# Fused attention and gated MLP on one Trainium2 core: batch 0's softmax and first layer split by tokens in place of heads, and a new order of all instructions

## The chip, the cores and the metric

The kernel runs on one core of a Trainium2 chip. The metric is the time of one execution on the device in microseconds (us), lower is better. The kernel before was run three times: 360.33, 360.48 and 363.59 us, a median of 360.48 us. The execution that was profiled took 361.51 us, and its first to last instruction span 359.7 us.

The engines are named as the profile does: PE is TensorE's matmul, PEld its weight load, DVE is VectorE, ACT is ScalarE, POOL is GpSimd, and SP issues the DMAs.

## The reference

B = 8 batches, H = 8 heads of D = 64, S = 512 tokens, Ns = 32 state rows, d_model = H·D = 512, d_ff = 1024.

```python
scores = x @ state.T / sqrt(D);  a = softmax(scores)      # over the 32 state rows, per token and head
xread  = a @ state                                        # (B, H, 512, 64)
scores2 = state @ x.T / sqrt(D); a2 = softmax(scores2)    # over the 512 tokens
sread  = a2 @ x                                           # (B, H, 32, 64)
X = concat([xread, sread], axis=2)                        # 544 rows per head, then heads side by side
h = relu(X @ w_in)                                        # (B, 544, 1024)
conv = conv_w[0]*h[t-1] + conv_w[1]*h[t] + conv_w[2]*h[t+1]
out = (h * sigmoid(conv)) @ w_out                         # (B, 544, 512)
```

## The kernel before

**How the work is cut.** `xread @ w_in` is not made in two steps: for each batch and each half of d_ff, u = state @ w_in is formed first (128 rows, 4 heads x 32 state rows, for each of two groups g of heads), and the hidden layer of 128 features f is then ps_h = u^T a (`hidden`, one step i = 8·b + f for each batch b and feature block f, 64 steps). A step goes on through ReLU, three taps of the convolution, tanh for the sigmoid, the gate, and four matmul groups, one for each chunk of 128 tokens, with w_out (`project`). Products at full accuracy are made of three passes in fp32r, a high part and a low part of each operand (`PASSES`); batch 0's first layer and its steps with i below `WHOLE` = 4 run instead as plain f32 matmuls, since their operands then need no split. The state rows (sread) are gathered for four batches at a time and go through the layers as "tails" (`state_hidden`, `tail`); the last token chunk of batch 0 goes through `last_product`.

**Weights.** w_in and w_out come in 16 pieces of 512 KB (`w_load`, tile raw) and each is converted by two ACT operations (L237, L240) and three DVE operations (L243, L246, L254) before PE may read it. w_in's columns are cut into four blocks of 1, 1, 2 and 4 feature blocks (`BLOCKS`), so that `block_state` can form batch 0's u for the first features before all of w_in is there.

**Batch 0's softmax.** The other batches take the softmax over state rows with DVE transposes (`softmax`). Batch 0 uses PE to be sooner (`first_softmax`): the scores (4 heads x 32 state rows on the partitions, 512 tokens along the free axis, one PSUM bank for each group g of four heads) are flipped (`first_flip`, L451), DVE takes the maximum for each token and head (`first_top`, L455), PE spreads it back into the bank of the scores (`spread`, L461, 16 matmuls), ACT takes the exponential (`first_exp`, L470), PE sums (`first_sum`, L474), DVE adds and inverts (`first_norm`, L478 and L479), PE spreads the inverses (L461 again, 16 matmuls), and DVE multiplies (`first_div`, L485). This chain is walked twice, once for each group g of heads. A step of the first layer (`hidden`, L588) adds both groups up, so that it needs both.

**What sets the order.** Each engine executes its instructions in the order of the program. The program's order is a table of numbers, `ORDER`: every operation is first listed with what it reads and writes (`add`), and the table then says in which order the operations are emitted; "-k" stands for k matmuls that fill PE's time (`fill`, L209) and a "v" after a number moves that operation from ACT to DVE. `Plan.order` refuses a table in which an operation stands ahead of one that it needs by that list. Buffers are few (`SBUF`): one buffer for a batch's x (xx), four for its transpose (xt), six for raw weights. All loads and stores are issued by SP, in order.

## Time and profile before

| | |
|---|---|
| median of three runs | 360.48 us |
| the profiled execution | 361.51 us |
| its span, first to last instruction | 359.7 us |
| granted TensorE clock, mean over the span | 0.995 |
| PE busy | 351.5 us (98%) |
| DVE busy | 319.6 us (89%) |
| ACT busy | 248.0 us (69%) |
| POOL busy | 67.6 us (19%) |
| DMA | 35.05 MB, mean 97 GB/s |

Of the chain of work that ended last, 92% of the span is PE and 6% DMA. The busiest group is the second layer (L651, 173.7 us on PE), then the first layer of batches 1 to 7 (L593, 83.9 us). In the first 50 us the 16 DMA engines are busy for 0.81 to 1.03 of the time. A busy PE is not a PE at its peak: its records overlap, and the start-to-start distance of a group's matmuls tells more than their durations. ACT and DVE instructions of a row that are merged (x2) show two starts and one end, so that half of such a row is what one of them adds to the queue.

### The profile page before, as it was taken

To read this page: it belongs to the slowest core of one execution; us is meant where nothing else is said; L and a number is where in the kernel's file an instruction comes from. 1 tells how busy PE (TensorE), PEld (TensorE's weight loads), DVE (VectorE), ACT (ScalarE), POOL (GpSimd) and SP (SyncE) were. 2 spreads that over 40 slices of the span, in tenths; PEclk is the share of its full clock that TensorE was granted. 3 is DMA by queue.
4 is the path that set the end of the run, shared out by engine and by line. 5 is a ranking of instruction groups with operands and counts; after the bars stand their busy time and mean duration, and the time that the engine had idled before them with its cause. 6 is when DMAs were issued, how large, how long until landed. Compare 5 with 4: busy or idle time off the path is not lost.

```text
span 359.7 us, 6635 instructions
## 1 busy us (share of the span) xinstructions
PE 351.5 (98%) x2488; PEld 266.0 (74%) x2488; DVE 319.6 (89%) x568; ACT 248.0 (69%) x506; POOL 67.6 (19%) x159
## 2 busy tenths in 40 slices
PE   7899999999999999999999999999999999999996
PEld 6644545878687877878878887887878777888884
DVE  1979999989999999999999999999799979998941
ACT  2789998998776889675784757656665555566541
POOL 1003100291301222111021402402202320410000
PEclk9989999999999999999999999999999999999999
DMA  7999886200443032300100002010030010100014
GB/s 260 389 356 379 282 342 236 104 2 1 148 148 118 0 126 79 133 17 2 68 21 29 2 6 81 2 59 3 0 117 2 0 58 2 59 1 31 30 58 146
DMA packets 12817, 35.05 MB, mean 97 GB/s; under 512 B 1521, under 2 KB 3697, under 8 KB 11761
## 3 DMA queue, kind: packets, MB, share of 16 engines
q1 hardware_dynamic: 12784, 34.63, 26.9%
q8 instruction: 19, 0.31, 0.4%
q14 instruction: 14, 0.11, 0.1%
HBM read 25.71 MB, written 8.91 MB: 96 GB/s over the span
## 4 chain that ended last, share of the span: by engine, by line
PE 92%; DMA 6%; SPq 0%; ACT 0%; issue 0%; DVE 0%; ACTq 0%; DVEq 0%
PE acc L651 45%; PE ps_h L593 21%; PE ps_hs L574 4%; PE ps_h L588 4%; PE ps_u L508 4%; PE acc_t L651 3%; DMA raw<-w_in 3%; PE ps_r L341 2%; DMA xx<-xn 2%; PE ps_s L300 2%; PE acc_c L651 2%; PE ps_t L328 1%; PE acc L659 1%; DMA raw<-conv_w 1%; PE ps_s L461 1%; PE ps_u L527 0%
## 5 line engine op out<-in xcount | busy, mean ns | idle before, releaser
L651 PE MATMUL acc<-wo,g 128*128 128x512 f32 x708 | 173.7, 393 | 0.0
L651 PEld LDWEIGHTS acc<-wo,g 128*128 128x128 f32 x708 | 130.9, 188 | 34.0 <-issue 4.2
L593 PE MATMUL ps_h<-a,u 128*128 128x512 f32 x336 | 83.9, 391 | 0.0
L593 PEld LDWEIGHTS ps_h<-a,u 128*128 128x128 f32 x336 | 62.6, 188 | 13.7 <-DVE u L202 0.8
L603 POOL COPY h<-hs 128x1 f32<-128x1 f32 x56 | 32.4, 588 | 166.4 <-DVE t L633 138.2
L628 ACT ACTIVATE t<-t 128x512 f32<-128x512 f32 x64 | 40.2, 632 | 19.9 <-DVE t L624 19.6
L624 DVE SCALAR_TENSOR_TENSOR t<-h,cw,t 128x512 f32<-128x512 f32 (+1 forms) x64 | 47.3, 745 | 1.1 <-DVE t L619 0.5
L633 DVE SCALAR_TENSOR_TENSOR t<-t,h 128x512 f32<-128x512 f32 (+1 forms) x64 | 42.4, 668 | 6.6 <-ACT t L628 6.4
L619 DVE SCALAR_TENSOR_TENSOR t<-h,cw,t 128x511 f32<-128x511 f32 x64 | 46.8, 743 | 1.0 <-ACT t L188 0.8
L608 POOL COPY hs<-h 128x1 f32<-128x1 f32 x64 | 29.2, 475 | 95.6 <-ACT h L194 87.2
L194 ACT ACTIVATE h<-ps_h 128x512 f32<-128x512 f32 x54 | 32.4, 599 | 19.4 <-PE ps_h L593 12.7
L199 ACT ACTIVATE g<-t 128x512 fp32r<-128x512 f32 (+1 forms) x60 | 37.0, 620 | 9.2 <-DVE t L633 7.7
L202 DVE TENSOR_TENSOR g<-t,g 128x512 fp32r<-128x512 f32 (+1 forms) x60 | 40.0, 675 | 1.1 <-ACT g L199 1.1
L188 ACT ACTIVATE t<-h,cw 128x512 f32<-128x512 f32 x49 | 34.8, 724 | 4.2 <-DVE g L202 2.3
L665 ACT ACTIVATE o<-acc 128x512 f32<-128x512 f32 (+1 forms) x29 | 15.8, 554 | 6.8 <-PE acc L651 4.9
L202 DVE TENSOR_TENSOR u<-ps_u,u 128x512 fp32r<-128x512 f32 x28 | 18.8, 682 | 0.6 <-ACT u L199 0.5
L574 PEld LDWEIGHTS ps_hs<-sr,wi 128*128 128x128 f32 x128 | 16.6, 191 | 3.2 <-ACT t L188 0.8
L199 ACT ACTIVATE u<-ps_u 128x512 fp32r<-128x512 f32 x28 | 16.0, 598 | 2.5 <-PE ps_u L508 2.4
L574 PE MATMUL ps_hs<-sr,wi 128*128 128x128 f32 x128 | 17.0, 276 | 0.0
L237 ACT ACTIVATE hc<-raw 128x512 f32<-128x512 f32 (+1 forms) x17 | 11.3, 666 | 7.6 <-DMA raw<-conv_w 4.4
L588 PE MATMUL ps_h<-p,u 128*128 128x512 f32 x32 | 14.8, 599 | 0.0
L508 PE MATMUL ps_u<-wi,st 64*32 64x512 f32 x224 | 14.8, 598 | 0.0
(95 smaller groups left out, 404.5 us busy)
## 6 DMA issues: line engine op xcount, KB each, us to landing
xt<-xT SPq DMA_DIRECT2D x16, 512.0 KB, 6.9
xx<-xn SPq DMA_DIRECT2D x8, 1024.0 KB, 4.9
out<-o SPq DMA_DIRECT2D x27, 256.0 KB, 2.1
raw<-w_in SPq DMA_DIRECT2D x8, 512.0 KB, 7.9
raw<-w_out SPq DMA_DIRECT2D x8, 512.0 KB, 7.9
out<-o SPq DMA_DIRECT2D x8, 128.0 KB, 1.8
out<-o_t SPq DMA_DIRECT2D x8, 64.0 KB, 1.7
st<-stT SPq DMA_DIRECT2D x1, 448.0 KB, 9.3
```

The lines of the kernel that those rows point to most:

```text
L188: A.activation(dst, src, AF.Copy, scale=scale)
L194: A.activation(dst, src, AF.Relu, scale=0.5)
L199: A.activation(hi, src, AF.Copy)
L202: engine.tensor_tensor(lo, src, hi.bitcast(F32), op=ALU.subtract)
L574: PE.matmul(ps_hs[m, f][:, :NT], wi[:, k, f * P:(f + 1) * P], sr[m][:, k, :], start=(k == 0), stop=(k == NK - 1))
L593: PE.matmul(ps_h[i], u[j][:, g, fs], a[k][:, g, :], start=(n == 0), stop=(n == 3 * NG - 1))
L603: G.tensor_copy(hd[i][:, S:], hs[m, f][:, j, 1:2])
L619: V.scalar_tensor_tensor(t[:, 1:], h[:, :S - 1], cw[:, f, 0:1], t[:, 1:], op0=ALU.mult, op1=ALU.add)
L624: V.scalar_tensor_tensor(t[:, :n], h[:, 1:n + 1], cw[:, f, 2:3], t[:, :n], op0=ALU.mult, op1=ALU.add)
L628: A.activation(tt[i], tt[i], AF.Tanh, scale=0.25)
L633: V.scalar_tensor_tensor(tt[i][:, :n], tt[i][:, :n], 1.0, hd[i][:, :n], op0=ALU.add, op1=ALU.mult)
L651: PE.matmul(acc, g[j][:, cs], wo[:, k, f, :], start=(f == 0 and n == 0), stop=(f == NF - 1 and n == 2))
```

## The change

The change has three parts.

1. Batch 0's two walks through `first_softmax` are no longer the two groups of heads; they are the two halves q of the tokens (`HS` = 256 tokens), each with all heads. The load of x transposed for batch 0 is cut in the same way (`xt_load`), the scores of a half go into two banks of 256 columns (`first_scores`), scaling, exponential and maximum work on 256 columns of each group, the inverses are spread into the bank of the flips, and the division is one DVE operation on 2 x 256 columns for each half. The first layer of batch 0 is cut in two as well (`first_hidden`): the matmuls of a token half need the division of that half alone. Each matmul there has 256 columns, and there are twice as many.
2. `WHOLE` goes from 4 to 2: steps 2 and 3 of batch 0 now split gate and w_out and run their second layer in three fp32r passes.
3. The list of needs is made exact (`join` writes one column and no longer the whole tile h; `flip` no longer claims e2t; `block_state` and the softmax of batch 0 name what they share), and the table `ORDER` is another one throughout: 36 operations carry a "v" where 33 did, and 13 fill matmuls stand in it where 18 did.

The core of the diff:

```diff
+HS = S // 2
+HC = NCH // 2
-WHOLE = 4
+WHOLE = 2
 ORDER = """
-120 121 0 98 -10 123 99 100 101 102 8 103 9 124v -6 141 2 11 10 125 3 149 126 142 12 -1 143 150 151 13 127 14 4 15 131
+120 0 -7 123 125v 121 98 99 100 101 -2 124 102 103 14 142 126 143 16 132 -2 150 2 20 15 144 3 4 8 151 145 127 152 17 5
...
     def xt_load(i):
         b, g = divmod(i, NG)
+        if b == 0:
+            xts[i] = buf([P, NP, HS], F32, "xt", f"xt_{i}")
+            nc.sync.dma_start(xts[i], xT[b, :, :, g * HS:(g + 1) * HS])
+            return
...
+    def first_scores(q):
+        if q == 0:
+            at[0] = buf([P, NG, S], F32, "at", "at_0")
+        ps_s[q] = [bank(f"ps_s_0_{q}_{g}") for g in range(NG)]
+        for j in range(NP):
+            for g in range(NG):
+                half = slice(g * D, (g + 1) * D)
+                PE.matmul(ps_s[q][g][j * NS:(j + 1) * NS, :HS], st[half, j, :], xts[q][half, j, :],
+                          start=True, stop=True)
+
+    def half_of(t, q):
+        return t[:, :, q * HS:(q + 1) * HS]
...
-    def first_exp(g):
+    def first_exp(q):
         if not pa:
             pa.append(buf([P, NG, S], F32, "at", "p_0"))
-        A.activation(pa[0][:, g, :], ps_s[g], AF.Exp, scale=SCALE)
+        for g, t in enumerate(ps_s.pop(q)):
+            A.activation(half_of(pa[0], q)[:, g, :], t[:, :HS], AF.Exp, scale=SCALE)
...
-    def first_spread(g):
-        spread(g, ident, True)
-
-    def first_div(g):
-        V.tensor_tensor(pa[0][:, g, :], pa[0][:, g, :], ps_s.pop(g), op=ALU.mult)
+    def first_spread(q):
+        spread(lambda k: ps_x[q][:, k * P:(k + 1) * P], q, ident, True)
+
+    def first_div(q):
+        V.tensor_tensor(half_of(pa[0], q), half_of(pa[0], q),
+                        ps_x.pop(q).rearrange("p (g s) -> p g s", s=HS), op=ALU.mult)
...
-        if b == 0:
-            for g in range(NG):
-                PE.matmul(ps_h[i], u[0][:, g, fs], pa[0][:, g, :], start=(g == 0), stop=(g == NG - 1))
-            return
...
+    def first_hidden(f, q):
+        if q == 0:
+            ps_h[f] = bank(f"ps_h_{f}")
+        for g in range(NG):
+            PE.matmul(ps_h[f][:, q * HS:(q + 1) * HS], us[0, f // 4][0][:, g, f % 4 * P:(f % 4 + 1) * P],
+                      half_of(pa[0], q)[:, g, :], start=(g == 0), stop=(g == NG - 1))
...
-            r = [("at", "p"), ("pa", 0), ("pa", 1), ("u0", 0, f // 4), ("uk", f, 0), ("uk", f, 1)]
+            for q in range(2):
+                add("PE", "hidden0h", partial(first_hidden, f, q), w=[("ps", "h", i)],
+                    r=[("at", "p"), ("pa", q), ("u0", 0, f // 4), ("uk", f, 0), ("uk", f, 1)])
...
-            add("POOL", "pool", partial(join, i), r=[("hs", m, f)], w=[("h2", i), h])
+            add("POOL", "pool", partial(join, i), r=[("hs", m, f), h], w=[("h2", i)])
```

The table moves instructions on every engine. Three places matter below. The rows are the built program's own; in a name such as hc_2_191 the first number is the tile's own (the weight piece, batch or step) and the last one counts buffers.

ACT, in the softmax of batch 0. hc and raw are a weight piece (0 and 1 hold w_in's first two blocks, 2 and 3 the third, 4 to 7 the fourth), p is the softmax of batch 0, and e2 the exponential of the other softmax, that over tokens. Before:

```order
L237 ACTIVATE hc_3_251<-raw_3_241 128x512
L240 ACTIVATE raw_3_241<-raw_3_241 128x512
L319 ACTIVATE e2_1_254,s2_1_255<-at_0_158,nm2_1_232 128x512
L240 ACTIVATE raw_2_227<-raw_2_227 128x512
L240 ACTIVATE raw_7_303<-raw_7_303 128x512
L237 ACTIVATE hc_5_308<-raw_5_305 128x512
L470 ACTIVATE p_0_234<-ps_s_0_1_139 128x512
```

And now:

```order
L502 ACTIVATE p_0_216<-ps_s_0_0_0_132 128x256
L502 ACTIVATE p_0_216<-ps_s_0_0_1_133 128x256
L238 ACTIVATE hc_3_248<-raw_3_189 128x512
L502 ACTIVATE p_0_216<-ps_s_0_1_0_154 128x256
L502 ACTIVATE p_0_216<-ps_s_0_1_1_155 128x256
L241 ACTIVATE raw_3_189<-raw_3_189 128x512
L341 ACTIVATE e2_0_261,s2_0_262<-at_0_131,nm2_0_219 128x512
L238 ACTIVATE hc_1_271<-raw_1_212 128x512
L341 ACTIVATE e2_1_286,s2_1_287<-at_0_131,nm2_1_178 128x512
L241 ACTIVATE raw_1_212<-raw_1_212 128x512
```

The second exponential of p stood behind work on the fifth and sixth pieces that are loaded (7 and 5); now both halves' exponentials stand ahead of the fourth loaded piece (1).

PE, from the second spread of inverses to batch 0's first layer. ps_x and ps_s are what the inverses are spread into, ps_t the flip of e, ps_h the first layer of one feature block. Before:

```order
L527 MATMUL ps_u_2_1_341<-wi,st 32x256
L461 MATMUL ps_s_1_139<-ident,s_1_334 32x128 x16
L300 MATMUL ps_s_0_378<-xt_312,st 32x512
...
L588 MATMUL ps_h_411<-p_234,u_0_279 128x512 x2
L588 MATMUL ps_h_416<-p_234,u_0_279 128x512 x2
```

And now:

```order
L561 MATMUL ps_u_2_1_298<-wi,st 32x256
L492 MATMUL ps_x_168<-ident,s_0_294 32x128 x16
L492 MATMUL ps_x_182<-ident,s_1_324 32x128 x16
L561 MATMUL ps_u_1_0_353<-wi,st 32x128
...
L350 MATMUL ps_t_366<-ident,e_1_286 128x128 x4
L631 MATMUL ps_h_378<-p_216,u_0_275 128x256 x4
L631 MATMUL ps_h_397<-p_216,u_0_275 128x256 x4
```

Both spreads now stand next to each other, behind the products with the third block of w_in, and the scores of the next batch (8 matmuls, L300) have left the place ahead of the first layer.

DVE, near the 230th of its 570 rows, in the steps of batch 2 (t_16 to t_23). u1_4 and u1_3 are low parts of u for batches 4 and 3, g1 the low part of a gate. Before:

```order
L202 TENSOR_TENSOR g1_16_1746<-t_16_1504,g0_16_1745 128x512
L202 TENSOR_TENSOR g1_17_1776<-t_17_1621,g0_17_1775 128x512
L322 TENSOR_SCALAR s2_12_1612<-s2_12_1612 128x1
L323 RECIPROCAL s2_12_1612<-s2_12_1612 128x1
L202 TENSOR_TENSOR u1_4_0_1715<-ps_u_4_0_1_1717,u0_4_0_1714 128x512
L633 SCALAR_TENSOR_TENSOR t_19_1654<-t_19_1654,h_19_1627 128x512
```

And now:

```order
L203 TENSOR_TENSOR g1_16_1739<-t_16_1637,g0_16_1738 128x512
L732 SCALAR_TENSOR_TENSOR ss_0_0_1355<-hs_0_0_82,cw_76,ss_0_0_1355 128x128
L444 TENSOR_SCALAR s1_3_1741<-s1_3_1741 128x32
L445 RECIPROCAL s1_3_1741<-s1_3_1741 128x32
L203 TENSOR_TENSOR g1_18_1754<-t_18_1614,g0_18_1753 128x512
L448 TENSOR_TENSOR af_3_1516<-af_3_1516,s1_3_1741 128x1024
L203 TENSOR_TENSOR u1_3_0_1762<-ps_u_3_0_1_1764,u0_3_0_1761 128x512
```

Batch 3's softmax (af_3) and u now come here, ahead of the rest of batch 2; the last row frees the PSUM bank into which PE's second chunk of batch 2's step 16 goes.

More of the change, by code (lines that the diff above doesn't have):

```diff
@@ L456, in first_top, with first_flip, spread @@
+    def first_flip(q):
+        ps_x[q] = bank(f"ps_x_{q}")
+        for k, g, cs in lumps(q):
+            PE.transpose(ps_x[q][:, k * P:(k + 1) * P], at[0][:, g, cs], ident)
+    def first_top(q):
+        sm[q] = buf([P, NCH, 4], F32, "s1", f"m0_{q}")
+        V.tensor_reduce(sm[q].rearrange("p c h -> p (c h)"), ps_x[q].rearrange("p (k n) -> p k n", n=NS), axis=AX.X,
                         op=ALU.max, negate=True)
-    def spread(g, by, start):
-        for c in range(NCH):
+    def spread(dst, q, by, start):
+        for k in range(NCH):
@@ L460, in spread @@
             for h in range(4):
-                PE.matmul(ps_s[g][h * NS:(h + 1) * NS, c * P:(c + 1) * P], sm[g][:, c, h:h + 1].broadcast_to([P, NS]), by,
-                          start=start and c == 0, stop=c == NCH - 1, skip_group_check=not start)
-    def first_shift(g):
-        spread(g, eight, False)
-    def first_exp(g):
+                PE.matmul(dst(k)[h * NS:(h + 1) * NS, :], sm[q][:, k, h:h + 1].broadcast_to([P, NS]), by,
+                          start=start and k == 0, stop=k == NCH - 1, skip_group_check=not start)
@@ L468, in first_exp, with first_shift @@
+    def first_shift(q):
+        spread(lambda k: ps_s[q][k // HC][:, k % HC * P:(k % HC + 1) * P], q, eight, False)
+    def first_exp(q):
         if not pa:
             pa.append(buf([P, NG, S], F32, "at", "p_0"))
[L470 to L479 removed]
@@ new lines, in first_softmax @@
+    def first_softmax(q):
+        x, m, n, p, e = ("ps", "x", q), ("s1", "m0", q), ("s1", "s0", q), ("pa", q), ("at", "p")
+        s = [("ps", "s", 0, q, g) for g in range(NG)]
+        add("PE", "flip", partial(first_flip, q), r=[("scores", 0, q), ("at", 0)], w=[x])
+        add("DVE", "red", partial(first_top, q), r=[x], w=[m])
+        add("PE", "spread", partial(first_shift, q), r=[m, ("scores", 0, q)], w=s)
+        add("ACT", "exph", partial(first_exp, q), r=s + [e] * q, w=[p] + [e] * (not q))
+        add("PE", "sum4", partial(first_sum, q), r=[p, e], w=[x])
+        add("DVE", "norm0", partial(first_norm, q), r=[x], w=[n])
+        add("PE", "spread", partial(first_spread, q), r=[n], w=[x])
+        add("DVE", "tt", partial(first_div, q), r=[x, e], w=[p])
@@ L847, in fused_kernel @@
         else:
-            for g in range(NG):
-                first_softmax(g)
+            for q in range(2):
+                first_softmax(q)
     for q in range(len(BLOCKS)):
```

137 lines of the change are left out of this document (64 added, 73 removed), and 57 rows, old and new, of the table ORDER.

## The prediction

> **What bounds the kernel now.** I read the page's first part, then the chain that ended last, then the engines' busy time by stretch, and last the timeline of the first 24 us.
>
> ```profile
> PE 351.5 (98%) x2488; PEld 266.0 (74%) x2488; DVE 319.6 (89%) x568; ACT 248.0 (69%) x506; POOL 67.6 (19%) x159
> ```
>
> The chain, in order of time (start, length, what):
>
> ```profile
> 7.86 9.78 DMA raw<-w_in
> 17.71 0.67 ACT hc L237
> 18.39 0.49 ACT p L470
> 18.92 1.05 PE ps_x L474 x8
> 19.98 0.93 PE ps_u L527 x16
> 20.91 1.86 PE ps_s L461 x32
> 22.77 1.38 PE ps_s L300 x16
> 24.15 5.35 PE ps_h L588 x12
> ...
> 29.50 1.02 PE ps_s L300 x16
> ...
> 41.52 0.86 PE acc L659 x2
> ...
> 63.54 0.70 PE acc L651 x3
> ...
> 350.08 6.13 PE acc L651 x27
> ```
>
> From 24.1 us, where batch 0's first layer starts, to 356.2 us the chain is PE at the pace of its matmuls, but for one load of x during which PE is busy as well. So the time is a start of 24.1 us, 332.1 us of PE, and a tail of 3.5 us. The start is set by the second walk of batch 0's softmax: its exponential (L470) stands on ACT behind a weight piece that lands at 17.7 us.
>
> PE is not alone. By stretches (length, then busy time and instructions of PE, PEld, DVE, ACT, POOL; clock; DMA share; GB/s):
>
> ```profile
> 23.44:137.60 114.16, 113.85 (x1013) 77.40 (x998) 111.28 (x203) 98.81 (x204) 27.27 (x52) 1.00 0.45 161
> 137.60:356.20 218.60, 218.59 (x1217) 174.04 (x1215) 194.71 (x336) 133.89 (x271) 38.58 (x84) 1.00 0.11 38
> 20.10:23.50 3.40, 3.40 (x56) 1.61 (x48) 2.51 (x8) 2.88 (x8) 0.00 (x0) 0.50 1.02 340
> 16.70:20.10 3.40, 1.81 (x20) 1.57 (x28) 2.52 (x6) 2.38 (x5) 0.00 (x0) 1.00 1.03 413
> 13.30:16.70 3.40, 2.85 (x75) 2.15 (x74) 2.68 (x8) 3.09 (x6) 0.00 (x0) 1.00 1.02 397
> ```
>
> For the 114 us behind the softmax DVE is idle for 2.9 us only: it is as full as PE. Later it has 24 us to spare. And just before the first layer PE ran at half clock for 3.4 us, after a stretch in which it was busy for 1.81 of 3.40 us.
>
> **The change part by part.** *PE's work* is nearly the same. Steps 2 and 3 have 6 matmul groups in the second layer (3 chunks each); each goes from 0.86 us (L659 above) to 0.70 (L651), so 6 x 0.16 = 1.0 us less. The scores that stood ahead of the first layer (L300, 1.02 us at full clock) now stand behind its start: 1.0 us more. The split matmuls stream as many columns as before. So from the first layer's start on PE has the same 332 us, and **what counts is when the first layer starts, and whether DVE can follow.**
>
> *The start.* The rows for the walk:
>
> ```profile
> 8.11 0.68 ACT L237 ACTIVATE hc<-raw 128x512 f32<-128x512 f32 x1 [1.34 <-DMA raw<-w_in]
> 13.48 0.69 ACT L237 ACTIVATE hc<-raw 128x512 f32<-128x512 f32 x1 [0.71 <-DMA raw<-w_in]
> 14.63 0.71 ACT L319 ACTIVATE e<-at,nm 128x512 f32<-128x512 f32 x1
> 15.34 1.23 ACT L240 ACTIVATE raw<-raw 128x512 uint32<-128x512 uint32 x2
> 20.95 0.55 ACT L188 ACTIVATE u<-ps_u 128x256 f32<-128x256 f32 x2 [0.38 <-PE ps_u L527]
> ...
> 14.54 1.08 PE L461 MATMUL ps_s<-ident,s 128*32 128x128 f32 x32
> 17.48 0.63 PE L328 MATMUL ps_t<-ident,e 128*128 128x128 f32 x4 [1.27 <-DVE p L485]
> ...
> 17.85 1.29 DVE L254 SCALAR_TENSOR_TENSOR wi<-raw,hc 128x512 uint32<-128x512 uint32 x2
> 20.01 0.18 DVE L478 TENSOR_SCALAR s<-ps_x 128x16 f32<-128x16 f32 x1 [0.88 <-PE ps_x L474]
> 20.22 0.25 DVE L479 RECIPROCAL s<-s 128x16 f32<-128x16 f32 x1
> 20.39 0.69 DVE L243 TENSOR_SCALAR hc<-hc 128x512 uint32<-128x512 uint32 x2
> ```
>
> The first and the fourth weight piece landed at 8.1 and 13.5 us, the third therefore near 11.7. The queue of loads is as long as before, but batch 0's x comes in runs of a quarter of the length; I allow 0.5 us for that (bounds 0 and 1), so third at 12.2, fourth at 14.0. From the third landing ACT's rows are: one weight operation (0.57), two exponentials of 256 columns (0.55), a weight operation (0.56): 13.9. Then DVE: one 0.60 operation and two more for the third block (15.7), a 0.34 shift, two inversions of 0.4 each (20.01 to 20.39, L478 and L479; 16.8). ACT meanwhile takes an exponential of 0.7, a weight operation, another exponential and a weight operation: 16.45. DVE: two 0.60 operations for the fourth piece and a small pair of 0.3 (L322 and L323, 131.41 to 131.68 below): 18.3; the division of the first half 18.9, a shift, the division of the second 19.85. PE: the third block's products end at 16.2, spreads of 0.93 each (L461) from 16.5 to 18.4, the second block's products 18.7, a flip of 0.5: 19.2. ACT has seven more operations on u and weights behind 16.45 (2.55 us): 19.0. **So the first layer starts at 19.3 us if the clock is full**, its second half's division done at 19.85 in time for it. With the clock halved a spread takes 1.86, as in the chain above: the spreads end at 20.2, the products and the flip at twice their length at 21.2, and the division at 20.95. [...] I take the middle: first layer at **20.2**, division at **20.4** (19.3 and 19.85 to 21.2 and 20.95), against 24.1 and 23.4.
>
> [...]
>
> *DVE behind the start.* The new order asks DVE for rows 32 to 230, 199 instructions, before PE may go into the second chunk of batch 2 (the third place shown above). From starts of neighbours:
>
> ```profile
> 31.96 1.41 DVE L624 SCALAR_TENSOR_TENSOR t<-h,cw,t 128x511 f32<-128x511 f32 x2
> 129.03 1.22 DVE L406 TENSOR_TENSOR af<-af,m 128x1024 f32<-128x1024 f32 x1
> 130.16 0.68 DVE L313 TENSOR_REDUCE nm<-at 128x1 f32<-128x512 f32 x1
> 131.41 0.14 DVE L322 TENSOR_SCALAR s<-s 128x1 f32<-128x1 f32 x1
> 131.68 0.73 DVE L624 SCALAR_TENSOR_TENSOR t<-h,cw,t 128x512 f32<-128x512 f32 x1
> 134.19 1.29 DVE L202 TENSOR_TENSOR g<-t,g 128x512 fp32r<-128x512 f32 x2
> ```
>
> a 512-column operation with one tensor of work adds 0.60 (L202), a tap 0.66 (L624), one of 1024 columns 1.13 (129.03 to 130.16). The 199 are 63 x 0.60, 52 x 0.66, 20 x 1.14, 14 of 384 columns at 0.47 (three quarters and a little of 0.60), 11 shifts at 0.34, and 39 small ones of 6.6 us together: 112 us. PE at that place has 215 us of matmuls left. PE had the same left at 137.6 us before, and DVE had by then done 111.3 us of work since the division (first of the stretches above). So the new order wants about 0.7 us more of DVE by the same point of PE, the two splits of gates among it, and everything 3 us earlier. DVE gets there at 20.4 + 112 + its idle time: with the 2.9 us of before 135.3, with half of it 133.9. PE itself would be there at 20.2 + 113.5 = 133.7. I take 134.6, nearer to the idle time seen. **The gain is 137.6 - 134.6 = 3.0 us** (bounds: 4.8 with the early start and a DVE that keeps up; 0.6 with the late start and 4 us of idle time, 20.95 + 112 + 4 = 137.0).
>
> *The rest.* Behind 137.6 us DVE is free for 24 of 219 us, so PE's 218.6 us stand. At the end two of the four last copies now run on DVE beside ACT:
>
> ```profile
> 352.83 0.76 DVE L667 TENSOR_SCALAR o<-acc 128x256 f32<-128x256 f32 x2 [0.94 <-PE acc L651]
> 356.23 0.66 ACT L665 ACTIVATE o<-acc 128x256 f32<-128x256 f32 x2 [0.70 <-PE acc L651]
> ```
>
> one of 0.42 in place of two in 0.66: 0.2 us less. Waits of PE that an order never run has elsewhere, on ACT between 25 and 50 us above all, I put at 0.3 us (bounds 0 and 2; the order before had 0.3, below). The exact needs cost nothing: POOL is busy for 19%.
>
> **Sum:** -3.0 - 0.2 + 0.3 = -2.9 us. The span goes from 359.7 to 356.8, that execution from 361.5 to 358.6, and the median of 360.5, 1.0 below the execution profiled, to **357.6 us**.
>
> **Rivals.** *PE alone binds.* DVE's idle time before fell where it had nothing to do; if it shrinks as DVE gets behind and the clock stays full, the first layer starts at 19.3 and PE is at the place at 132.8: 4.8 + 0.2 less, 355.5 us. Against it: DVE was 97% busy in that stretch already.
>
> *The clock halves over the spreads.* Start 21.2, division 20.95; DVE 20.95 + 112 + 2.9 = 135.9, so 1.7 + 0.2 less and 0.3 more: 358.9 us. [...]
>
> *The single buffer of x.* PE's read of x (L341) stands in its queue, with all behind it; each load can be issued only when the read before it is through.
>
> ```profile
> 51.02 1.10 PE L341 MATMUL ps_r<-xx,e2t 128*32 128x64 f32 x64 [0.31 <-DMA xx<-xn]
> DMA to landing us min/median/max: 4.8/4.9/8.7
> ```
>
> By the matmuls between them, PE gives the loads about 9, 6.0 and 6.9 us in the new order (6 to 7 before). At the median nothing is late. At the worst time seen, 8.7 us, two are late by 2.7 and 1.8; with the first read, for which 8.7 MB must have landed some 8.8 us into the first layer, late by 2 as well, PE loses 6.5 us: 364 us, slower than before. It decides from a loss of 2.9. For it: DMA is full until 50 us and now wanted earlier. Against: in the trace of before the one that came late did so by 0.31 us, and the next two loads queue behind less than then.
>
> *The split doesn't bring the start forward*, because the first layer also needs u of its features, and these hang on weights, not on the softmax: no change, 360.4 us. Against: the four pieces have landed by 14.0.
>
> **How the numbers follow.** The forecast, DVE setting the pace behind an earlier start, gets 0.5, with its own range of 356.2 to 359; PE alone 0.2; the halved clock 0.16; x late 0.1; no earlier start 0.04. A measurement of this kernel tells about 1% from no change, 3.6 us: faster means below 356.9, slower above 364.1. Faster takes all of the first rival and a third of the forecast, 0.37; slower half of the third rival's chance less a little, 0.04; the rest, 0.59, is within 1%. The range that leaves out no more than 2 in 10 reaches from the first rival's 355.4 to 361.0, short of the worst case of x.
>
> **What would show it.** Right: L631 starts between 19.3 and 21.2 us with the exponentials of both halves before 14 us; DVE is idle for less than 3 us between the division and 135 us; PE waits for DVE near 130 us, for one or two us in all; PE's work from the first layer on is 332 us. Wrong: first layer behind 22 us (the start's sum fails); PE at its pace throughout with DVE in hand (first rival); half clock over L492 (second); PE waiting at L363 for xx (third); PE waiting for ACT between 25 and 60 us by more than 2 us (the term for other waits fails).

## The result, and the profile after

The changed kernel takes 359.72 us (median of 20 runs, 358.7 to 363.0) against 362.3 us for the kernel before on the same chip (20 runs, 359.7 to 365.6). The ratio is 0.994, with a 95% interval of 0.9914 to 0.9966: 0.6% less, some 2.2 us, or between 1.2 and 3.1 (the two medians lie 2.6 apart). The forecast was 2.9 us less, from a median of 360.48 that three runs had given; from there to 362.3 are 1.8 of the 2.1 us by which the forecast time of 357.6 lies too low. The profiled executions differ by less: 361.51 to 360.01 us, span 359.7 to 358.2. **So in the profile 1.5 us are gained where 2.9 were forecast,** and the question is where the rest of a start that came 3.7 us earlier went.

A part of the timed gain is the clock's. Each run has its mean granted clock on record, and 0.995 is what one stretch of 3.4 us at half clock leaves, as in the profile of the kernel before (20.1 to 23.5 us). The changed kernel's profile has one as well (15.1 to 18.5 us), and a mean of 0.993, since its clock falls again behind PE's last matmul (0.80 in the mean from 353.75 us to the end). Over all comparisons below, on several chips, the kernel before took 360.8 us in the 28 runs with a mean clock of 0.998 or more and 362.5 us in the 54 with 0.994 or 0.995; the changed kernel took 359.4 us in 11 runs and 359.9 us in 20 (0.992 to 0.995). These are medians without an interval. At full clock the gain is about 1.4 us, with one halved stretch 2.6: a halved stretch cost the kernel before 1.7 us and the changed one 0.5.

The first part of the page of the changed kernel:

```profile
PE 350.4 (98%) x2532; PEld 272.4 (76%) x2532; DVE 323.0 (90%) x574; ACT 248.5 (69%) x508; POOL 46.6 (13%) x159
```

PE is at 98% as before; such a share doesn't tell of 1 or 2 us. I therefore cut PE's time at two marks that both programs have: the first layer's first matmul (L631, before L588), and the first matmul of the state tokens (L609, before L574). By stretches (length, then busy time of PE, PEld, DVE, ACT, POOL; clock; DMA share; GB/s), first the kernel before, then the changed one:

```profile
24.08:62.48 38.40, 38.09 (x444) 18.14 (x437) 37.63 (x80) 36.98 (x80) 4.73 (x14) 1.00 0.86 311
62.48:356.20 293.72, 293.71 (x1777) 233.29 (x1775) 267.72 (x459) 195.72 (x395) 61.12 (x122) 1.00 0.14 50
```

```profile
20.37:59.97 39.60, 39.45 (x492) 25.59 (x491) 37.53 (x79) 37.76 (x85) 5.24 (x14) 1.00 0.94 355
59.97:353.72 293.75, 293.65 (x1777) 233.26 (x1776) 272.43 (x465) 197.48 (x395) 39.69 (x122) 1.00 0.14 49
```

Behind the state tokens both take the same 293.7 us. The first layer comes 3.71 us earlier, the stretch up to the state tokens is 1.20 longer, and behind PE's last matmul 4.5 us follow where there were 3.5: -3.71 + 1.20 + 0.03 + 0.98 = -1.50. The stretch that got longer is the one in which the loads run at 355 GB/s and 94% of the DMA engines' time, against 311 and 86% before.

The chain of waits of the changed kernel, where it answers to the one shown of before:

```profile
17.60 0.60 DVE wi L255
18.62 8.19 DMA xt<-xT
26.85 1.06 PE ps_s L305 x8
27.92 2.79 PE ps_h L631 x12
30.70 1.03 PE ps_r L363 x64
...
60.14 7.14 PE ps_hs L609 x64
...
134.06 1.13 DVE af L448
...
135.84 6.44 PE acc L689 x27
...
344.20 9.53 PE acc L689 x42
353.76 0.39 ACT o L703
354.18 0.42 DVE o L705
```

The chain does not begin at the first layer any more. It runs through a load of x, issued at 18.62 us behind a weight load that had waited for DVE, and landed at 26.8. DVE's softmax of batch 3 stands in it at 134 us, as forecast. The timeline shows what waits for loads around 25 us:

```profile
24.25 0.68 ACT L241 ACTIVATE raw<-raw 128x512 uint32<-128x512 uint32 x1 [1.10 <-DMA raw<-w_out]
24.99 0.71 ACT L189 ACTIVATE t<-h,cw 128x512 f32<-128x512 f32 x1
25.67 2.25 PE L305 MATMUL ps_s<-xt,st 64*32 64x512 f32 x16
25.73 0.75 DVE L657 SCALAR_TENSOR_TENSOR t<-h,cw,t 128x511 f32<-128x511 f32 x1 [1.14 <-ACT t L189]
26.85 0.15 PEld L305 LDWEIGHTS ps_s<-xt,st 64*32 64x32 f32 x8 [1.05 <-DMA xt<-xT]
30.63 0.47 PEld L363 LDWEIGHTS ps_r<-xx,e2t 128*32 128x32 f32 x29 [0.33 <-DMA xx<-xn]
```

Three engines wait for the queue of loads: ACT 1.10 us for a piece of w_out, DVE behind ACT 1.14, PE 1.05 for x. The matmuls' own row hides PE's wait (its ends are modelled: 16 matmuls in 2.25 us that otherwise take 1.02), the row of the weight loads shows it.

### The profile page after: what moved, and what is told of

It is laid out like the page before. It is cut to its first block, busy times and chain, and to the rows that moved or that the text cites. A ratio compares the mean times of both kernels' runs of the same rounds, so it can differ in the third digit from the quotient of the medians.

```text
span 358.2 us, 6725 instructions
## 1 busy us (share of the span) xinstructions
PE 350.4 (98%) x2532; PEld 272.4 (76%) x2532; DVE 323.0 (90%) x574; ACT 248.5 (69%) x508; POOL 46.6 (13%) x159
## 4 chain that ended last, share of the span: by engine, by line
PE 90%; DMA 4%; DVE 4%; issue 0%; ACT 0%; SPq 0%; DVEq 0%
PE acc L689 46%; PE ps_h L624 21%; PE ps_hs L609 4%; DMA xt<-xT 4%; PE acc_t L689 3%; PE ps_u L542 3%; PE ps_h L631 3%; PE ps_r L363 2%; PE ps_s L305 2%; PE ps_t L350 2%; PE acc_c L689 2%; PE acc L697 1%; DVE hc L247 1%; DVE wi L255 1%; DVE hc L244 0%
## 5 line engine op out<-in xcount | busy, mean ns | idle before, releaser
L689 PE MATMUL acc<-wo,g 128*128 128x512 f32 x726 | 179.0, 394 | 0.1
L689 PEld LDWEIGHTS acc<-wo,g 128*128 128x128 f32 x726 | 134.5, 188 | 33.5 <-issue 3.0
L624 PE MATMUL ps_h<-a,u 128*128 128x512 f32 x336 | 82.9, 390 | 0.0
L646 POOL COPY hs<-h 128x1 f32<-128x1 f32 x64 | 24.1, 390 | 191.5 <-ACT h L195 172.8
L189 ACT ACTIVATE t<-h,cw 128x512 f32<-128x512 f32 x47 | 33.5, 722 | 1.0 <-DVE g L203 0.8
L641 POOL COPY h<-hs 128x1 f32<-128x1 f32 x56 | 16.6, 312 | 75.1 <-DVE t L671 55.8
L238 ACT ACTIVATE hc<-raw 128x512 f32<-128x512 f32 (+1 forms) x17 | 11.6, 681 | 5.8 <-DMA raw<-conv_w 5.5
L609 PEld LDWEIGHTS ps_hs<-sr,wi 128*128 128x128 f32 x128 | 14.7, 192 | 1.0 <-ACT h L195 0.8
L631 PE MATMUL ps_h<-p,u 128*128 128x256 f32 x64 | 15.1, 386 | 0.0
L609 PE MATMUL ps_hs<-sr,wi 128*128 128x128 f32 x128 | 14.9, 276 | 0.0
L631 PEld LDWEIGHTS ps_h<-p,u 128*128 128x128 f32 x64 | 11.8, 190 | 4.0 <-issue 0.8
```

Source lines behind the costliest of these rows:

```text
L189: A.activation(dst, src, AF.Copy, scale=scale)
L609: PE.matmul(ps_hs[m, f][:, :NT], wi[:, k, f * P:(f + 1) * P], sr[m][:, k, :], start=(k == 0), stop=(k == NK - 1))
L624: PE.matmul(ps_h[i], u[j][:, g, fs], a[k][:, g, :], start=(n == 0), stop=(n == 3 * NG - 1))
L631: PE.matmul(ps_h[f][:, q * HS:(q + 1) * HS], us[0, f // 4][0][:, g, f % 4 * P:(f % 4 + 1) * P], half_of(pa[0], q)[:, g, :], start=(g == 0) ...
L689: PE.matmul(acc, g[j][:, cs], wo[:, k, f, :], start=(f == 0 and n == 0), stop=(f == NF - 1 and n == 2))
```

## The experiments

Each kernel's time stands against the kernel before, run beside it on the same chip. Of the kernel before a fifth to a half of the runs beside it were at full clock, and these are 1.7 us faster than those with one halved stretch, so a difference of a few tenths of a per cent between rows is not clear. For every profile I give the first layer's start, the stretch up to the state tokens, the stretch from there to PE's last matmul, and the tail behind it, all read like the stretches above (us):

```
                 start   to L609   to last PE   tail   time / before (95%)
before           24.08   38.40     293.72       3.5    1
changed          20.37   39.60     293.75       4.5    0.9940 (0.9914 to 0.9966)
after_again      19.85   40.37     293.77       4.5    0.9944 (0.9921 to 0.9967)
whole            20.08   42.68     293.75       4.5    0.9990 (0.9962 to 1.0018)
scores_later     20.47   40.18     293.76       4.5    0.9977 (0.9952 to 1.0002)
act_later        22.29   38.73     293.78       4.5    0.9945 (0.9918 to 0.9972)
loads_order      19.66   40.21     293.76       4.5    0.9926 (0.9899 to 0.9954)
half_loads       20.50   38.41     293.77       4.5    0.9904 (0.9868 to 0.9939)
dve_more         20.40   38.72     294.69       4.5    0.9965 (0.9938 to 0.9991)
dve_less         20.57   39.29     293.77       4.5    0.9944 (0.9914 to 0.9975)
best1            19.51   40.01     293.73       4.5    0.9925 (0.9894 to 0.9956)
before_exp       22.26   41.82     293.74       3.5    1.0005 (0.9969 to 1.0041)
before_half      22.54   38.15     293.77       3.5    0.9955 (0.9918 to 0.9991)
best2            19.80   41.50     293.77       4.8    0.9976 (0.9945 to 1.0006)
```

My first theory was the prediction's, refined: PE and DVE come to the place at 135 us nearly together, and each loses about a microsecond on the way. The rivals were that PE alone binds and that DVE alone does. The first four kernels were made for these.

**The changed kernel again.** No edit.

> The changed kernel once more, as the measure for the three beside it. In its profile the first layer started at 20.4 us, PE was at the place (second chunk of batch 2, behind DVE's low part of u for batch 3) at 135.8, and its last matmul ended at 353.7, 333.4 us behind the first layer's start. What hangs on the order of the work must come again: a wait of about 1.1 us of PE for a load of x behind the first layer's first matmuls, one of 1.1 us of ACT for a piece of w_out, 115.5 us from the first layer to the place. What hangs on the phase of the clock (half clock from 15.1 to 18.5 us) and on the last stores (4.5 us from the last matmul to the end) may differ. Time against the kernel before: 0.991 to 0.997.

PE's wait for x came again (1.0 us) and a second one with it (0.9 us, for batch 0's x); ACT's wait for w_out did not (it waited 0.5 us for a piece of w_in), and from the first layer to the place it took 116.3 us. What I had not expected: the clock stayed full (0.999 in the mean), the first layer started 0.52 us earlier, and the state tokens still came 0.25 us later (19.85 + 40.37 = 60.22, against 59.97). An earlier start that is worth nothing can be a sign of something that doesn't depend on the start.

**The first layer's matmuls whole.**

```diff
-            PE.matmul(ps_h[f][:, q * HS:(q + 1) * HS], us[0, f // 4][0][:, g, f % 4 * P:(f % 4 + 1) * P],
-                      half_of(pa[0], q)[:, g, :], start=(g == 0), stop=(g == NG - 1))
+            PE.matmul(ps_h[f], us[0, f // 4][0][:, g, f % 4 * P:(f % 4 + 1) * P], pa[0][:, g, :],
+                      start=(g == 0), stop=(g == NG - 1))
```

(all of it at q = 0; at q = 1 the function returns)

> The first layer's matmuls of batch 0 at 512 columns, as before the change, in place of two of 256; everything else as changed. Theory of two limits: PE and DVE come to the place within 0.4 us of each other, DVE the later; the 256-column matmuls (0.2325 us, against 0.4296 for 512) cost PE 0.8 to 1.1 us, but taking this back alone leaves DVE as it is: first layer to the place 115.2 to 115.5, time 0 to 0.3 us less. Theory that PE alone binds: the full price, place 0.8 to 1.1 us earlier, time 0.8 to 1.1 us less. Theory that the halves cost nothing: no change in the busy time of those matmuls (14.5 us).

All of these are wrong about the time, which went up by about 0.5% against the changed kernel. From matmul to matmul the halves take 0.216 us each (median in the changed kernel), the whole ones 0.429: the halves cost next to nothing (0.432 against 0.429). The 0.2325 us of my expectation lies above that median. The chain of this kernel shows one wait:

```profile
19.32 0.43 SPq L234
19.80 12.05 DMA xx<-xn
31.89 1.10 PE ps_r L363 x64
```

The read of batch 0's x (L363) starts when x has landed, 12 us after it was asked for. Why the loads of this version came so late is not shown; only that PE had to wait for them.

**The scores later, and ACT's work on w_out later.** In the table of the order 202 to 204 are the scores of batch 2 and their copies, 52 is ACT's rounding of the first w_out piece.

```diff
scores_later:
-192 200 202 203 521 43 531 493 502 204 522 532 503 48
+192 200 521 43 531 493 502 522 532 503 202 203 204 48
act_later:
-490 517 52 450 519 530 44 45 129 520 47 491 51 46 189
+490 517 450 519 530 44 45 129 520 47 491 51 46 52 189
```

> The scores of batch 2, for which PE waited about 1.1 us for a load of x at 25.7 us, stand behind the first layer's matmuls of step 1 (2.8 us later in PE's queue), and their two copies on ACT with them. Theory of two limits: PE's wait goes, but DVE still comes to the place as late, so time 0 to 0.3 us less. Theory that PE alone binds: 1.1 us less. If the copies come later for DVE's reduction of the maxima, DVE gets a new wait near 29 us: time the same or up to 0.5 us more.

> ACT's rounding of the first w_out piece, for which ACT waited 1.1 us at 24.25 us and with it DVE 1.14 us at 25.7 for ACT's multiplication by the taps, stands three operations later in ACT's queue. Theory of two limits: DVE's idle time goes (1.1 us less of it up to 30 us), and then PE's own losses bind: first layer to the place 114.9 to 115.2, time 0.3 to 0.6 us less. Theory that DVE alone sets the place: place 1.1 us earlier, time 1.1 us less. Theory that PE alone binds: 0 to 0.35 us less.

Without its place in PE's queue the wait for x was gone at 25 us, but DVE had a new one of 1.85 us (for the copies of these scores) and the stretch was no shorter, 40.18 us. With ACT's rounding moved, the stretch was 38.73 us, but behind a start of 22.29: there the clock was halved for 6.8 us ahead of it. Start and stretch together, the state tokens come at 60.65 and 61.02 us. So far five profiles of the changed order had starts from 19.85 to 22.29 us, 2.4 us apart; but for `whole` (62.8) they reached the state tokens between 59.97 and 61.02, and in all five PE's read of batch 0's x started within 0.1 us of its landing. From there on all take 293.75 to 293.78 us, whatever happened ahead. That speaks against the theory of two limits at the place: DVE's and PE's losses on the way to 135 us would have to show behind the state tokens. The new theory: **the loads set the pace up to the state tokens.** Its rival was still DVE.

**Loads and DVE set against each other.** `half_loads` leaves out half of the bytes of x for batches 1 to 7 and of the other layout of x; `dve_less` leaves out a tap; `dve_more` does four operations twice.

```diff
half_loads:
-        nc.sync.dma_start(xts[i], xT[b, :, 2 * g:2 * g + 2, :])
+        nc.sync.dma_start(xts[i][:, :1], xT[b, :, 2 * g:2 * g + 1, :])
-        nc.sync.dma_start(xxs[b], xn[b])
+        nc.sync.dma_start(xxs[b][:, :2], xn[b, :, :2])
dve_less, in before(i):
+        if 8 <= i < 12:
+            return
dve_more, in w_low(f):
-        low(wo[:, 1, f, :], whole[f], wo[:, 0, f, :])
+        for _ in range(2 if 2 <= f < 6 else 1):
+            low(wo[:, 1, f, :], whole[f], wo[:, 0, f, :])
```

> The changed kernel with half of the x of batches 1 to 7 and half of the other layout of x left out (each load has half the bytes, and the matmuls read the half that is there twice), so that every instruction is as before but the loads are lighter. Theory of loads: x for the scores of batch 2 lands about 1.2 us earlier, batch 0's other layout 2 to 3 us earlier; PE waits for neither, L609 comes at 58.2 to 58.9 us, and the time falls by 1 to 1.8 us. Theory of DVE: 0 to 0.6 us less (only what ACT and DVE wait for w_out at 24 us). If the loads were no limit at all: no change.

> The first of the two convolution taps of steps 8 to 11 is left out (part of the computation: these four steps lack a tap), 4 x 0.66 = 2.6 us less of DVE's work between 65 and 110 us. Theory that DVE alone sets the place: PE there 2.0 to 2.6 us earlier, and the time as much less. Theory that PE and DVE are level there: PE's wait of 0.36 us goes and no more, 0.2 to 0.4 us less. Theory of loads: 0 to 0.4 us less, since PE's work between L609 and the place is what it is.

> Four of DVE's operations on w_out (the low parts of pieces 2 to 5, 0.6 us each, near 56 to 70 us) are done twice, with the same result: 2.4 us more of DVE's work before the place. Theory that DVE sets the place: 2.4 us less the 1.1 us that it idles behind them at 111 and 120 us, so PE at the place 1.3 to 2.4 us later and the time 1.3 to 2.4 us more. Theory of loads, with DVE in hand behind 60 us: less than 0.5 us more.

With the light loads the stretch fell to 38.41 us, within 0.01 of what it took in the kernel before, and the time to 0.9904 (four runs; the interval overlaps with that of the changed kernel):

```profile
20.50:58.91 38.41, 38.41 (x492) 25.52 (x491) 37.47 (x79) 37.70 (x85) 5.26 (x14) 1.00 0.70 232
58.91:352.68 293.77, 293.66 (x1777) 233.14 (x1776) 272.61 (x465) 197.43 (x395) 39.65 (x122) 1.00 0.12 39
```

That is what the theory of loads says, at the lower end of its numbers (1.1 us in the profile), and DVE's work is the same 37.5 us as in the changed kernel. But the loads of one profile differ from those of the next: `dve_more`, whose loads are whole and in the changed order, took 38.72. So the reading rests on more than one pair. Without a wait PE reads batch 0's x 9.07 us behind the first layer (`half_loads`, 20.50 to 29.57). These are the profiles with PE's order unchanged (us):

```
                 start   x landed   read of x   L609
half_loads       20.50   27.88      29.57       58.91
dve_more         20.40   29.73      29.77       59.12
dve_less         20.57   30.48      30.53       59.86
changed          20.37   30.57      30.63       59.97
after_again      19.85   30.63      30.67       60.22
act_later        22.29   31.60      31.64       61.02
```

With whole loads the read begins within 0.06 us of the landing in all five, and the state tokens follow the read by 29.3 to 29.6 us in all six. Whether the first layer starts at 19.85 or at 22.29, what arrives at L609 arrives when x does.

With a tap left out in four steps (DVE's work behind the state tokens falls from 272.43 to 270.16 us), PE reached the place in the same time behind the state tokens, 75.84 us against 135.84 - 59.97 = 75.87; in the stretch up to the place, and in DVE's timeline at 111 us, first of `dve_less`, then of the changed kernel:

```profile
59.86:135.70 75.84, 75.77 (x511) 58.94 (x510) 71.83 (x119) 61.90 (x121) 12.81 (x41) 1.00 0.23 77
```

```profile
108.75 0.71 DVE L664 SCALAR_TENSOR_TENSOR t<-h,cw,t 128x512 f32<-128x512 f32 x1
111.37 0.69 DVE L673 SCALAR_TENSOR_TENSOR t<-t,h 128x512 f32<-128x512 f32 x1 [1.91 <-ACT t L668]
```

```profile
111.49 0.69 DVE L671 SCALAR_TENSOR_TENSOR t<-t,h 128x512 f32<-128x512 f32 x1 [0.58 <-ACT t L666]
```

DVE waits 1.91 us there in place of 0.58: it has nothing to do until PE and ACT bring the next step. So DVE does not set the place. It is not far from it either: of 2.4 us more in `dve_more` (two of the four operations stand ahead of the state tokens), 0.94 came out behind them (293.75 to 294.69). That is between what the two theories expected, under 0.5 and 1.3 or more.

**Another order of loads.** Of the table's numbers 200 is a load of x for batch 2, 44 the last piece of w_in, 50 and 56 the first two of w_out, 122 the other layout of x for batch 0; ACT's 52 moves as above.

```diff
-199 13 50 448 27 34 ... 517 52 450 519 530 44 45 129 520 47 491 51 46 189 192 200 202 ... 56 122 137
+199 200 13 448 27 34 ... 517 450 519 530 44 50 122 45 129 520 47 491 51 46 52 189 192 202 ... 56 137
```

> The changed kernel with another order of loads: batch 2's second piece of x goes out ahead of the last piece of w_in and the first of w_out, batch 0's other layout of x ahead of the second piece of w_out, and ACT rounds the first piece of w_out three operations later. Theory of loads: in five versions PE's read of batch 0's x began within 0.1 us of the landing of x, and from the first matmul of the state tokens (L609) to PE's last one all took 293.8 us; so what a version gains is made before L609, at the pace of the loads. Then PE's wait for x at 25.7 us (1.1 us) goes, x lands 1.2 us earlier, L609 comes at 58.6 to 59.2 us (59.97 and 60.22 before), and the time falls by 0.8 to 1.4 us. Theory that DVE sets the place whatever the loads do: L609 earlier, but PE waits longer behind it, 293.8 becomes 294.6 to 295.0, time 0 to 0.4 us less.

Half right. Both waits of PE went, and the read of x began at 28.84 us; but the stretch stayed at 40.21 us, since ACT now waited 0.77 us, up to 26.20 us, where the piece of w_out (landed at 26.12) and one of DVE's taps (ended at 26.16) came together, and PE's next flip waited for ACT in its turn. What one load gained, another gave back. The time is 0.9926 of before; the interval overlaps with that of the changed kernel.

**The kernel before, started earlier, and with light loads.** 152 to 156 are the second walk of batch 0's softmax, from its exponential to its division.

```diff
before_exp:
-144 -1 145 20 5 17 129 6 21 22 132 146 147 16 23 7 444 18 447 148 1 44 ... 24 19 152 134 153 25 ... 445 154 35 ... 449 156 38
+144 152 -1 145 20 5 17 129 153 6 21 22 132 146 154 147 155 16 23 7 444 18 447 148 156 1 44 ... 24 19 134 25 ... 445 35 ... 449 38
-        add("DVE", "tt", partial(first_div, g), r=[s], w=[p, ("at", "p")])
+        add("DVE", "tt", partial(first_div, g), r=[s], w=[p])
```

(`before_half` is the edit of `half_loads` in the kernel before; in both the x of batch 0's scores stays whole.)

> The kernel before with batch 0's softmax still split by heads, but with the second walk's exponential straight behind the first one on ACT, ahead of the weight pieces, and its sums, inversion, spread and division brought forward with it (the need that the second exponential follows the first division is taken out, since the data don't have it). The start as the prediction reasoned, set by the second walk behind a weight piece: the first layer comes at 21.0 to 22.5 us in place of 24.1. Theory of loads: of these 2 us a half or more is lost again at the loads of x up to L609 (62.5 us in the kernel before), so 0.3 to 1.2 us less time. If nothing behind the start held PE back: 1.6 to 3 us less. If the start hangs on u and the loads and not on the exponential: first layer at 23 to 24.1, no change.

> The kernel before with half of the x of batches 1 to 7 and half of the other layout of x left out (the half that is there is used twice). Theory of loads, by which the loads hold PE back only once it starts earlier: from the first layer to L574 (state tokens) 38.4 us were all PE's work but for one wait of 0.3 us, so that stretch gets 0.1 to 0.4 us shorter; the first layer itself may come up to 1 us earlier where weights land earlier. Rival, that the loads hold any version back by as much: 1 to 1.4 us between the first layer and the state tokens, as in the changed kernel. Tail 3.5 us as in the kernel before, against 4.5 in all versions of the changed one.

Without any split, the first layer of `before_exp` starts 1.8 us earlier than in the profile of the kernel before; the stretch behind it grows by 3.4 us, and the state tokens come 1.6 us later (64.08 against 62.48; ratio 1.0005). Its chain shows where:

```profile
23.28 11.54 DMA xx<-xn
34.86 1.15 PE ps_r L341 x64
36.02 7.84 DMA xx<-xn
43.99 1.14 PE ps_r L341 x64
45.15 7.34 DMA xx<-xn
52.62 1.10 PE ps_r L341 x64
```

This is a closed loop: read, then the next load into the single buffer, 7 to 8 us until it has landed, the next read. PE is through with the work between two reads before the load lands.

Two things keep this from being a clean test of an earlier start. The first is the clock, which was full in `before_exp` and in `before_half` and halved for 3.4 us in the profile of the kernel before. `before_half` leaves the exponential where it stood, and still its first layer starts at 22.54 us:

```profile
18.37 0.49 ACT p L471
18.90 1.06 PE ps_x L475 x8
19.96 0.59 PE ps_u L528 x16
20.55 1.04 PE ps_s L462 x32
21.59 1.02 PE ps_s L301 x16
22.61 5.35 PE ps_h L589 x12
```

In the kernel before the exponential comes at the same 18.39 us, and the last three rows ahead of the first layer take 0.93, 1.86 and 1.38 us in place of 0.59, 1.04 and 1.02. So 1.5 of the 1.8 us are the clock, and about 0.3 us (22.54 to 22.26) is left for the exponential; that it alone held the start is not shown. The second is that the loads of `before_exp` came later themselves: the last piece of w_in was asked for at 17.2 us in place of 15.4, and batch 0's x landed at 34.8 in place of 33.2, though asked for 1.3 us earlier. Run by run, `before_exp` took 362.9 us at full clock (7 runs) and 362.8 with one halved stretch (4 runs), the kernel before beside it 361.0 and 362.6 (5 and 13 runs). So at full clock the moved exponential costs 1.8 us, and in this version, where the loads hold PE back, the clock ahead of them is worth nothing either. With light loads (`before_half`) the stretch takes 38.15 us in place of 38.40, as expected.

**A better version?** `best1` is `loads_order` with the first w_out piece's work later on ACT and DVE, and with the last of the output's copies back on ACT. `best2` also sends one load of x (323) ahead of a load of the other layout (160) that waits for a read, and two of the eight last stores on ACT's queue.

```diff
best1:
-491 51 46 52 189 192 202 203 521 43 531 493 502 204 522 532 503 48 53 49 ... 240 205 206 158 159 54 210 211 193 492
+491 46 189 192 202 203 521 43 531 493 502 204 51 52 522 532 503 48 49 ... 240 205 210 193 53 54 206 158 159 211 492
-1513v 1514
+1513 1514
best2:
-217 160 512 174 180 323
+217 323 160 512 174 180
-        nc.sync.dma_start(out[b, c * P:(c + 1) * P, parts_of(b, c)[q]], outs.pop((b, c, q)))
+        (nc.scalar if (b, c) == (B - 1, 2) else nc.sync).dma_start(
+            out[b, c * P:(c + 1) * P, parts_of(b, c)[q]], outs.pop((b, c, q)))
```

> The version with the other order of loads (loads_order), and in it the work on the first w_out piece moved once more (on ACT behind the two copies of batch 2's scores, on DVE behind the maxima of batch 2 and the low part of u), because there ACT still waited 0.8 us for that piece and DVE 0.7 and 0.55; and the last of the eight copies of the output back on ACT. Theory of loads: PE's work without a wait for loads needs 38.4 us from the first layer to L609 (half_loads; the kernel before the same), loads_order took 40.2; if the rest of the waits hung on that piece, 38.6 to 39.4 us, L609 at 58.6 to 59.4, time 0.5 to 1.2 us less than loads_order. Rival: the next load in the row is late instead, and L609 stays at 59.8. Tail, from PE's last matmul to the end: 4.5 us in all versions of the changed kernel; with both halves of the last chunk on ACT 4.2 to 4.4 if DVE's wait for ACT's copy and the issue of the last store behind it set it.

> The last version (best1: other order of loads, work on the first w_out piece later) with two more moves: one load of x for batch 5 goes out ahead of the third load of the other layout, which sits on SP until PE has read the one before (in that wait the loads ran at 206 GB/s between 40 and 45 us, against 350 to 417 beside it), and the two stores of the first finished chunk go out on ACT's queue in place of SP's. Theory of loads: the loads behind 44 us land 1.2 us earlier, the scores of batches 4 and 5 wait 0.4 us less, L609 0.3 to 0.8 us earlier than 59.5 us; rival: the third load of the other layout is later by as much and its read waits, no change. Tail: all versions of the changed kernel had 4.5 us, also with the last copy back on ACT, which falls the idea that DVE's wait for that copy sets it; if SP sets it, which sends eight stores of 0.45 to 0.5 us each one behind the other up to 1.4 us behind PE's end (0.9 in the kernel before), two stores fewer give 0.5 us less: 3.9 to 4.1. If not, 4.5. Time 0.3 to 1.1 us less than best1.

`best1` is 0.4 us better than `loads_order` in the profile and the same in time (0.9925): most of its waits did not hang on that piece. `best2` lost it again, by the rival that was named for it; its chain:

```profile
41.76 1.08 PE ps_r L363 x64
42.86 7.03 DMA xx<-xn
50.02 1.10 PE ps_r L363 x64
```

The load of x that went ahead took the queue, and the load that closes the loop landed at 49.9 us in place of 46.6 (asked for at 42.9 in place of 41.8).

On the tail both told something. With the last copy on ACT the tail was still 4.5 us, so DVE's copy is not its cause. The timelines point to the stores; no version here shortened the tail. In the timeline of the changed kernel, of the one before and of `best2`, the last stores on SP (start, length, count):

```profile
351.72 3.79 SPq L723 DMA_DIRECT2D out<-o  x8
```

```profile
352.63 4.82 SPq L685 DMA_DIRECT2D out<-o  x8
```

```profile
353.07 0.85 ACTq L723 DMA_DIRECT2D out<-o  x2
353.98 0.39 ACT L703 ACTIVATE o<-acc 128x256 f32<-128x256 f32 x1 [0.93 <-DVE o L705]
354.39 2.80 SPq L723 DMA_DIRECT2D out<-o  x6
```

PE's last matmul ends at 353.72, 356.20 and 355.07 us. The changed order finishes its chunks so close together that the eight stores go out one straight behind the other, 0.47 us each on average, and the last is through 1.8 us behind PE; before, SP waited for copies in between and was through 1.25 behind PE. In `best2` six stores follow each other as closely, but the first of them waits for a copy of ACT that stands behind ACT's two stores, and the last is through 2.1 us behind PE. That accounts for 0.5 us of the tail. Another 0.4 lies behind the last landing: from there to the last instruction are 1.3 us in the profile of the changed kernel and 0.9 in that of the kernel before, with POOL's last one 1.3 and 0.8 us behind the landing; why is open.

## Why the prediction was right or wrong

**The start** came out as forecast, in part by luck. Forecast was 20.2 us for the first layer (19.3 to 21.2) and 20.4 for the last division; the profile has 20.37, and a division from 19.72 to 20.40. Both halves' exponentials were over by 13.3 us. The 0.5 us that was allowed for batch 0's x, which comes in pieces of a quarter of the length, is a term that no run shows: the third and the fourth weight piece landed at 11.7 and 13.5 us, where 12.2 and 14.0 were forecast, and at 11.6 and 13.4 in the kernel before. The clock was halved from 15.1 to 18.5 us, over the spreads, but that cost less than reckoned: with it the start lies at 20.4 to 20.6 in five profiles, without it at 19.5 to 20.1 in five others (21.2 and 19.3 were expected). The luck is on the other side of the difference: the 24.1 us of the kernel before were read from one profile, and 1.5 of them are its halved stretch (`before_half`, at full clock: 22.54). The prediction weighed a halved clock only for the new order. At full clock the start moves from there to between 19.5 and 20.1, by 2.5 to 3.0 us.

**PE's work** was right: 332 us from the first layer on, unless it waits. `half_loads` has 38.41 + 293.77 = 332.18.

**DVE behind the start** is the step that failed. Its arithmetic held: 112 us of work were forecast for rows 32 to 230, and DVE was busy for 111.8 between the first layer and the place. But I took the place, at which DVE is the last to come, for something that DVE's whole load sets. `dve_less` shows that it isn't: 2.3 us less work behind the state tokens, the place as late. PE was to lose one or two us to DVE near 130 us, and behind the state tokens it lost 0.03 us against before. What held PE back stood ahead of them: the read of batch 0's x, which began within 0.06 us of the landing of x in five profiles. Of its idle time (3.7 us, where the sign was under 3) 2.3 us were waits for ACT, at 25.7, 56.4 and 111.5 us. The place came at 135.84 us and not at 134.6. As a mark it was also less exact than I thought: PE had 217.9 us before its end there (the prediction counted 215), and 218.6 at 137.6 us before. The state tokens are the better mark, and there the gain is 62.48 - 59.97 = 2.5 us.

**Other waits of PE** is the term that should have been large: 0.3 us, with the worry put on ACT. By the stretch up to the state tokens 1.2 us were lost in the first profile of the changed kernel and 2.0 in the second, nearly all of it to loads of x that PE waited for: the read of batch 0's x came 1.2 and 1.8 us later than 9.07 us behind the first layer. The forecast let 0.9 us of the start go to DVE and 0.3 to these waits, 1.2 together. That sum agrees with the first profile by luck; its cause is another one.

**The tail** had the wrong sign: -0.2 forecast, +1.0 measured. I counted the two copies and not the stores that queue on SP behind them. These 1.2 us are nearly all that lies between the forecast of 2.9 and the 1.5 in the profile; the rest is 0.2 us of the start (-3.7, forecast -3.9).

**The rivals.** The one of the single buffer of x came nearest, and of it only the first read: PE read batch 0's x as it landed, at 30.6 us. The loop behind it did not hold the changed kernel back. The next three loads landed at 39.4, 47.6 and 56.1 us and were read at 41.4, 48.7 and 56.7; it is in `before_exp` that the loop binds. The rival got a chance of 0.1, since at the median landing time of before (4.9 us) nothing was late, and was priced with the worst one at 6.5 us, of which 2 were the first read's. The time to landing did not stay what it was: asked for earlier, with the DMA engines busy for 94% of the time up to the state tokens, against 86% before, the loads of the other layout of x took 6.0 us in the median. And the loads did not keep the pace that the prediction left them with. Between 15 and 24 us, first the kernel before, then the changed one:

```profile
15.00:24.00 9.00, 6.92 (x132) 3.92 (x123) 6.55 (x14) 6.84 (x16) 0.00 (x0) 0.81 1.01 378
```

```profile
15.00:24.00 9.00, 9.00 (x135) 7.05 (x134) 8.23 (x21) 7.46 (x18) 0.78 (x2) 0.81 0.90 276
```

The changed order moved 276 GB/s there in place of 378 (321 in `after_again`); why is not shown. The clock did halve over the spreads, as the second rival said, without the loss it reckoned behind them: a start 0.5 us later reached the state tokens 0.25 earlier. What makes the clock halve no run here shows, so that this rival's chance of 0.16 was my estimate alone. That PE alone binds is felled by the waits, and that the start doesn't move by 20.37.

Timed over many runs the gain is 2.2 us with an interval that holds 2.9, and 359.72 us lies within the range of 355.4 to 361.0; the reason that was given for the size did not hold.

## What to carry to other kernels

Before you price an earlier start, ask whether the loads behind it would be earlier too: here the DMA engines were busy for 94% of the time up to the state tokens, batch 0's x was read within 0.06 us of its landing in five profiles, and what was gained ahead of that read was at risk up to there. A time from issue to landing that was measured in one order need not hold in another (here 4.9 us became 6.0, and 4.2 with half the bytes); work with the bytes ahead in the queue, and with closed loops (a single buffer, read, load, read: 7.8 and 7.3 us a load in `before_exp`), instead. Look at the granted clock before you take a start from one profile: here 1.5 of the 3.7 us between two starts were a halved stretch in one of them. And cut the span at marks that both programs share: that one stretch came out at 293.7 to 293.8 us in all but one of the profiles told at once where not to look.

## What the runs showed of the hardware

In the changed kernel the half clock came after a stretch in which PE's records cover almost everything:

```profile
11.70:15.10 3.40, 3.18 (x24) 2.77 (x24) 3.40 (x8) 3.40 (x10) 0.00 (x0) 1.00 1.00 391
15.10:18.50 3.40, 3.40 (x65) 2.37 (x68) 2.98 (x11) 2.91 (x7) 0.00 (x0) 0.50 0.86 290
```

3.18 of 3.40 us look busy, but by 24 matmuls only, 16 of them with four columns (L506); in the kernel before a stretch with 1.81 us and 20 matmuls was followed by it too, and one with 2.85 us and 75 matmuls was not. Counting busy time of the profile was therefore not enough here to tell whether the clock would fall. The halved stretch ahead of the first layer was absent in five profiles of the changed kernel and its versions, 3.4 us long in five, and 6.8 us in one (`act_later`, from 13.6 to 20.4 us); the same program had it in one execution and not in the next (`after_again`; mean clocks of 0.993 and 0.999).

Stores of 128 KB cost SP 0.40 to 0.53 us each to send (from one start to the next, in the changed kernel), and eight in a row were through 1.8 us behind PE's last matmul. Sending the eight takes SP 3.8 us at the very end of the program, and moving two of the stores to ACT cost ACT 0.85 us ahead of a copy that the others waited for; the tail was 4.8 us there in place of 4.5.
